# The first batch's attention heads in whole float32 products instead of split ones

## Chip, cores, metric

One core of one Trainium2 chip. The metric is the device time of one execution in microseconds, lower is better.

## What is computed

Block-causal attention over 8 batches of 8 heads (576 positions, 64 dimensions), then, per batch, the real part of a two-dimensional Fourier transform added to the attention's output, a normalization and a two-layer network with ReLU:

```python
scores = scale * np.matmul(q, k.transpose(0, 1, 3, 2))
scores = np.where(mask, scores, -1000000000.0)      # mask: 64-blocks, causal
attn = np.exp(scores - np.max(scores, axis=-1, keepdims=True))
attn = attn / (np.sum(attn, axis=-1, keepdims=True) + 1e-09)
out = np.matmul(attn, v)
...
X = np.fft.fft(np.fft.fft(x, axis=1), axis=2)
u = x + np.real(X)
un = (u - mu) / np.sqrt(var + 1e-06)
return u + np.maximum(un @ w_ch1, 0.0) @ w_ch2
```

q, k and v are float32, the network's weights float64.

## The kernel before

No product is done in float32 as such. An operand is split into a leading part and what is left, each in a type that TensorE takes in one pass, and the products of the parts are added in PSUM.

- **Scores.** `load_head` brings q and k of a head (64 rows, 1152 columns) into a tile `raw`. `lead` (ScalarE) rounds them to float32r in a tile `LEAD`, which also holds eight rows of a mask and a ninth for the row maxima. `rest` subtracts, q's half on VectorE and k's on GpSimd, into a tile `REST` of 128 rows, whose other halves get copies of the lead parts by two DMAs (`lead_copies`). `max_part` multiplies lead by lead with the mask (72 rows) for the row maxima, `shift` turns the maxima on TensorE and puts them by DMA into row 73 of `LEAD`, and `scores` makes each piece of the scores, transposed, as a product of `REST` (128 rows) plus one of `LEAD` (73 rows).
- **Probabilities.** ScalarE takes the exponential twice, into f16 (`ph`) and into float32 (`p32`); GpSimd subtracts to make the low part `pl`.
- **Values.** V of a pair of heads is scaled by a power of two from its sum of squares (`sum_v`, `split_v`, with a product by a matrix of ones on TensorE) and split into f16 parts `VH` and `VL`. `values` makes 15 blocks a head, each as three f16 products: `ph` with `VH`, `ph` with `VL`, `pl` with `VH`. VectorE then normalizes into `x`, and a DMA stores it to a scratch tensor `xd`.

`NB = 3` heads have `LEAD` and `REST` tiles at a time. When all eight heads of a batch are in `xd`, its transform starts: `mirror` gathers rows by DMA, `fourier_steps` does the rest, and `feed_steps` the network in f16 parts. The network's float64 weights are loaded by DMAs that ScalarE issues, `weight_single` turns them into float32 by bit operations on VectorE (`W`), and `weight_parts` makes f16 parts; for the first matrix ScalarE and GpSimd do this, and it waits for the scale of the whole matrix. Heads of batch 1 and later wait until the first matrix is ready.

The order of instructions on each engine is set when the program is built: a planner takes steps from several lanes (`head_lane`, `prepare_lane`, `v_lane`, `max_lane`, `score_lane`, `value_lane`, `transform_lane` and the weights' lanes), each step with a cost on TensorE and a chain of costs on other engines, and writes out the one that is due next. Each engine then runs its instructions in that order. All products are recorded at lines L216 and L219, all other engines' work at L194.

Of the kernel before, what the change touches and what calls it, by code (L numbers as in the profile page):

```python
# [200 lines left out]
def tile_attn_fourier_ffn(  # L201
# [43 lines left out]


    NB = 3
    LEAD = [const.tile([KS, 64 + 2 * S], F32R, name=f"lead{i}") for i in range(NB)]
# [3 lines left out]
    VH = [const.tile([P, 5, 2, D + 1], F16, name=f"VH_{i}") for i in range(2)]  # L252
    VL = [const.tile([P, 5, 2, D], F16, name=f"VL_{i}") for i in range(2)]
    ZT = const.tile([34, NCOS], F32R, name="ZT")
    for i in range(NB):
        gpsimd.dma_start(LEAD[i][D:KS], c_masks)
        vector.tensor_scalar(LEAD[i][0:D, 0:64], ones[0:D, 0:64], 0.0, None, op0=ALU.mult)
    for i in range(2):
        vector.memset(VH[i][:, 0:4, :, D:D + 1], 1.0)
        vector.memset(VH[i][0:64, 4, :, D:D + 1], 0.0)  # L260
        vector.memset(VH[i][64:128, 4, :, D:D + 1], 1.0)
# [90 lines left out]

    def load_head(h):

        raws[h] = work.tile([D, 2 * S], F32, name="raw", bufs=2)
        sync.dma_start(raws[h], qk[h])
        yield

    def lead(h):
        scalar.copy(LEAD[h % NB][0:D, 64:], raws[h])  # L360
        yield

    def lead_copies(h):
# [12 lines left out]
        yield  # L376

    def load_v(g):
        V = vraw[g] = work.tile([P, 5, 2, D], F32, name="V", bufs=1)
        sync.dma_start(V.rearrange("p c h d -> p (c h d)"), v[g])  # L380
        yield

    vraw = {}
# [9 lines left out]
    def split_v(g):  # L393

        acc = vsums.pop(g)
        V = vraw.pop(g)
        t = ps_tile()
        mm(t[:, 0:1], ones, acc[:, 0:1], start=True, stop=True)
        yield
        sc = acc[:, 2:3]  # L400
        x = work.tile([P, 1], I32, name="pw", bufs=2)
        vector.tensor_copy(acc[:, 1:2], t[:, 0:1])
        vector.tensor_scalar(
            x, acc[:, 1:2].bitcast(I32), 0x7F000000, 1, op0=ALU.bitwise_and, op1=ALU.logical_shift_right
        )
# [3 lines left out]
        scalar.activation(vh[:, :, :, 0:D], V, AF.Copy, scale=sc)  # L409
        yield  # L410
        vector.scalar_tensor_tensor(vl, V, sc, vh[:, :, :, 0:D], op0=ALU.mult, op1=ALU.subtract)
        pairs[g] = sc
        yield

    def head_lane():
        for h in range(B * H):
            yield Step(
                lambda: load_head(h), 0.0, ("Q0.6", "M1.0", "L2.0"), (("T2", h - 2, 0), ("T2", h - 2, 1)) if h > 1 else (), ("L", h), place=h - 2.2
            )

    def prepare_lane():
        for h in range(B * H):
            yield Step(
                lambda: lead(h), 0.0, ("A1.15",), (("L", h),), ("T", h), place=h - 1.0,
                need=(("S", h - NB, 2),) if h >= NB else (),
            )
            yield Step(lambda: lead_copies(h), 0.0, ("Q1.2", "M1.0", "L1.6"), (("T", h),), ("TC", h), place=h - 0.9)
            yield Step(lambda: rest(h, 0), 0.0, (_x(S),), (("T", h),), ("T2", h, 0), place=h - 0.8)
            yield Step(lambda: rest(h, 1), 0.0, (_g(S),), (("T", h),), ("T2", h, 1), place=h - 0.8)

    def v_lane():
        for g in range(B * H // 2):
            yield Step(
                lambda: load_v(g), 0.0, ("Q0.6", "M1.1", "L2.0"), (("N", g - 1),) if g else (), ("LV", g), place=2 * g - 2.2,
            )
            yield Step(lambda: sum_v(g), 0.0, ("t1", "A0.95", "t"), (("LV", g),) + ((("V", 2 * g - 3, 4),) if g > 1 else ()), ("NS", g),
                       place=2 * g - 0.6)
            yield Step(
                lambda: split_v(g), 0.11, ("D0.46", "B", "A0.83", "X0.88"), (("NS", g),), ("N", g), True,
                need=(("V", 2 * g - 3, 4),) if g > 1 else (), place=2 * g - 0.4,  # L440
            )

    def max_part(h, n):

        m = M[h % 2]
        x = LEAD[h % NB][0:KM]
        kh = x[:, 64 + S:]
        qh = lambda j: x[:, P * j:P * (j + 1)]
# [23 lines left out]
    def shift(h):  # L472

        t = ps_tile()
        tp(t[0:5, 0:P], M[h % 2][:, 0:5], ident)
        yield
        mt = work.tile([5, P], F32R, name="mt", bufs=2)
        scalar.activation(mt, t[0:5, 0:P], AF.Copy, bias=float(8.0 * PSHIFT * np.log(2.0)), scale=-1.0)
        yield
        dst = LEAD[h % NB][KM:KS, 0:640].rearrange("r (j p) -> r j p", j=5)  # L480
        sync.dma_start(dst.bitcast(F32), mt.bitcast(F32))
        yield

    probs = {}
# [9 lines left out]
    def scores(h, n):  # L494
# [2 lines left out]
        i, at, chunks = PIECES[n]  # L497
        if at == 0:
            width = S if i == 0 else 512
            probs[h, i] = [work.tile([P, width], F16, name=f"p{x}{i}", bufs=1) for x in "hl"]  # L500
        ph, pl = probs[h, i]
        t = ps_tile()
        w = 0
        for c, lo, width in chunks:
            first, last = P * c + lo, P * c + lo + width
# [16 lines left out]
    def values(h, at):  # L522
# [8 lines left out]
        ph, pl = probs[h, tile_]  # L531
        for j in range(c, 5):

            lo = col + P * (j - c) - (64 if j == 4 else 0)
            for i, (lhs, rhs, w) in enumerate((
                (ph, vh[:, c, hh], D + 1), (ph, vl[:, c, hh], D), (pl, vh[:, c, hh], D + 1)
            )):
# [13 lines left out]
        den, sc = DEN[h % 2], pairs[g]  # L551
        eps = 1e-9 * 2.0 ** PSHIFT
        vector.tensor_scalar(den, av[:, :, D], eps, sc, op0=ALU.add, op1=ALU.mult)
        rec = work.tile([P, 5], F32, name="rec", bufs=2)
        vector.reciprocal(rec, den)
        vector.tensor_tensor(
            x[:, :, hh], av[:, :, 0:D], rec.unsqueeze(2).to_broadcast([P, 5, D]), op=ALU.mult
        )
        yield
        if hh == 1:  # L560
# [7 lines left out]
    def score_lane():  # L568
        for h in range(B * H):
            for n, (i, at, chunks) in enumerate(PIECES):  # L570
                w = sum(x[2] for x in chunks)
                yield Step(
                    lambda n=n: scores(h, n), w / 1200.0, (_a(w), "p1", _a(w), "B", _g(w), "p"),
                    (("X", h), ("TC", h), ("T2", h, 0), ("T2", h, 1)), ("S", h, i) if n else None, True,
                    need=(("V", h - 1, 2 * i),) if h else (), place=h,
                )

# [373 lines left out]
    def weight_load(x):  # L951

        i, n, at = LANDS[x]
        if x < 2:
            vector.tensor_copy(raw(x)[0:1, 0:1].bitcast(F32), raws[x][0:1, 0:1])
            yield
        scalar.dma_start(raw(x).rearrange("p (j n) -> p j n", j=n), weight(i, n))
        yield
# [52 lines left out]
    def load_lane():  # L1011

        for x, (i, n, at) in enumerate(LANDS):
# [1 line left out]
            after = tuple(("WS", y) for y in {x - FLIGHT, *same} if y >= 0) + ((("WL", x - 1),) if x else ())  # L1015
            yield Step(
                lambda: weight_load(x), 0.0, (("D0.2",) if x < 2 else ()) + ("A0.45", f"M{1.8 * n}", "L2.0"),
                (("LV", 0), ("L", x)) if x < 2 else after, ("WL", x),
            )

    def weight_lane(w):
# [147 lines left out]
```

## Time and profile before

| | |
|---|---|
| median of 3 runs | 1278.12 us (1277.02 to 1279.54) |
| span of the profiled execution | 1275.3 us, 25121 instructions |
| that execution's own time | not given apart from its span |
| TensorE products | 1181.1 us busy (93%) |
| VectorE, ScalarE, GpSimd | 703.5 (55%), 548.7 (43%), 523.6 us (41%) |
| mean granted TensorE clock | 0.947 |
| first batch's heads, batch 0's transform, the rest | to about 93 us, to about 172 us, to the end |

In the profile's rows PE is a product on TensorE, PEld a load of its stationary operand, DVE VectorE, ACT ScalarE, POOL GpSimd, SP the queue that issues most DMAs. A product's row starts when it begins to stream and ends when its results are out, so neighbouring rows overlap, and the distance of starts is what a product costs in a row of them.

### The profile page before, as it was taken

What the parts mean: (1) busy time and instruction counts of PE and PEld (TensorE: products, weight loads), DVE (VectorE), ACT (ScalarE), POOL (GpSimd) and SP (SyncE); (2) the same over time, 40 slices, a digit from 0 to 9 for tenths busy, and PEclk for the clock granted to TensorE, in tenths of its full rate; (3) what the DMA queues carried; (4) which work ended last, traced back from release to release, by engine and by line L of the source; (5) the groups of instructions that cost most, each with busy time, mean ns of one, the idle gap of its engine ahead of it and who ended that gap; (6) DMA issues with size and microseconds to landing.
All of it is one profiled execution on the core that took longest, in us unless ns stands there. A gap on an engine that the chain in (4) does not pass through costs nothing.

```text
span 1275.3 us, 25121 instructions
## 1 busy us (share of the span) xinstructions
PE 1181.1 (93%) x10068; PEld 892.9 (70%) x10068; DVE 703.5 (55%) x1433; ACT 548.7 (43%) x1137; POOL 523.6 (41%) x593
## 2 busy tenths in 40 slices
PE   5772598999799999999999999999999999999998
PEld 5672376677677777777777777777777667766665
DVE  6787777756747574664546573557445414422211
ACT  5655647554444555534645545454443112111110
POOL 4664944454643654563534644446441400300000
PEclk9655688999899999999999999999999999999999
DMA  7674242342223233232323232413220100000000
GB/s 210 201 243 156 80 140 70 87 111 52 74 71 109 62 81 86 79 75 54 93 75 95 65 90 68 111 51 87 77 74 10 40 19 19 21 17 1 17 17 17
DMA packets 56371, 99.07 MB, mean 78 GB/s; under 512 B 7757, under 2 KB 26653, under 8 KB 56256
## 3 DMA queue, kind: packets, MB, share of 16 engines
q1 hardware_dynamic: 49152, 73.16, 21.2%
q10 hardware_dynamic: 4384, 16.78, 4.0%
q0 software_dynamic: 2720, 7.54, 2.1%
q8 instruction: 79, 1.29, 0.4%
q14 instruction: 36, 0.29, 0.1%
HBM read 58.46 MB, written 18.87 MB: 61 GB/s over the span
## 4 chain that ended last, share of the span: by engine, by line
PE 80%; DVE 10%; POOL 3%; issue 3%; DMA 2%; ACT 1%; SPq 0%; DVEq 0%; POOLq 0%; ACTq 0%
PE acc L216 28%; PE h L216 27%; PE ps L216 17%; PE av L216 6%; DVE W L194 2%; DVE M L194 2%; DVE tmp L194 2%; PE ps L219 2%; POOL u L194 1%; DMA lead<-mt 1%; DVE VL L194 1%; POOL W L194 1%; POOL pl L194 1%; DVE rest L194 1%; POOL ag L194 0%
## 5 line engine op out<-in xcount | busy, mean ns | idle before, releaser
L216 PE MATMUL h<-uh,W 128*128 128x256 f16 x2304 | 431.4, 275 | 2.7 <-DVE M L194 2.3
L194 POOL TENSOR_TENSOR pl<-p,ph 128x288 f16<-128x288 f32 (+1 forms) x256 | 253.7, 1002 | 355.6 <-ACT p L194 167.8
L216 PEld LDWEIGHTS <-W 128*128 128x128 f16 x3456 | 325.8, 99 | 64.9 <-issue 6.3
L216 PE MATMUL acc<-W,gh 128*128 128x512 f16 x1104 | 329.8, 380 | 0.0
L216 PE MATMUL h<-ul,W 128*128 128x256 f16 x1152 | 315.8, 274 | 0.0
L194 DVE TENSOR_REDUCE M<-ps 128x1 f32<-128x448 f32 (+3 forms) x292 | 131.9, 484 | 181.3 <-PE ps L216 180.5
L194 ACT ACTIVATE gh<-h 128x512 f16<-128x512 f32 x138 | 82.3, 597 | 305.1 <-PE h L216 302.3
L216 PE MATMUL ps<-lead 72*128 72x64 f32 (+9 forms) x700 | 201.3, 346 | 9.2 <-ACT lead L194 6.8
L216 PE MATMUL acc<-W,gl 128*128 128x512 f16 x552 | 209.2, 379 | 0.0
L194 DVE SCALAR_TENSOR_TENSOR gl<-h,gh 128x512 f16<-128x512 f32 x138 | 94.6, 687 | 200.9 <-ACT gh L194 200.8
L194 ACT ACTIVATE ph<-ps 128x512 f16<-128x512 f32 (+1 forms) x233 | 117.5, 506 | 146.9 <-PE ps L216 144.3
L216 PEld LDWEIGHTS <-gh 128*128 128x128 f16 x1104 | 96.7, 98 | 80.1 <-issue 4.7
L216 PEld LDWEIGHTS ps<-lead 72*128 72x128 f32 (+1 forms) x700 | 128.0, 202 | 18.3 <-ACT lead L194 6.8
L216 PEld LDWEIGHTS <-ph 128*128 128x128 f16 x1920 | 113.5, 104 | 31.1 <-ACT left L194 4.9
L216 PE MATMUL ps<-rest 128*128 128x320 f32 (+3 forms) x350 | 124.0, 361 | 1.4 <-ACT p L194 0.8
L216 PE MATMUL av<-VH,ph 128*128 128x65 f16 x960 | 118.1, 203 | 6.1 <-DVE x L194 6.1
L194 ACT ACTIVATE p<-ps 128x512 f32<-128x512 f32 (+1 forms) x233 | 117.2, 505 | 4.3 <-POOL pl L194 2.8
L216 PE MATMUL av<-VH,pl 128*128 128x65 f16 x960 | 116.6, 201 | 1.8 <-POOL pl L194 1.4
L216 PE MATMUL av<-VL,ph 128*128 128x64 f16 x960 | 117.2, 201 | 0.0
L194 POOL TENSOR_TENSOR rest<-raw,lead 64x576 fp32r<-64x576 f32 x64 | 96.9, 1514 | 15.1 <-ACT lead L194 9.5
L216 PEld LDWEIGHTS <-gl 128*128 128x128 f16 x552 | 54.0, 98 | 66.2 <-DVE gl L194 1.7
L216 PEld LDWEIGHTS <-pl 128*128 128x128 f16 x960 | 94.8, 103 | 2.7 <-POOL pl L194 2.5
(169 smaller groups left out, 1435.4 us busy)
## 6 DMA issues: line engine op xcount, KB each, us to landing
raw<-in_qk_dram SPq DMA_DIRECT2D x64, 288.0 KB
rest<-lead SPq DMA_DIRECT2D x128, 144.0 KB
W<-in_moe_w_ch_dram ACTq DMA_DIRECT2D x14, 1024.0 KB
V<-in_v_dram SPq DMA_DIRECT2D x32, 320.0 KB
xd<-x SPq DMA_DIRECT2D x32, 256.0 KB
out_dram<-u SPq DMA_DIRECT2D x32, 256.0 KB
u<-xd SPq DMA_DIRECT2D x8, 512.0 KB
u<-in_moe_w_ch_dram ACTq DMA_DIRECT2D x4, 512.0 KB
```

What stands on the lines that cost most here:

```text
L194: x = f(*args, **kw)
L216: return tc.keep_in_program_order(nc.tensor.matmul(*args, **kw))
L219: return tc.keep_in_program_order(nc.tensor.transpose(*args, **kw))
```

## The change

For the eight heads of batch 0 alone, `h < H`:

- q and k are loaded straight into `LEAD`, now a float32 tile; `lead` writes their float32r rounding into `REST`, with masks of its own, and `max_part` works on that. No rest is made and nothing copied.
- `scores` is one float32 product a piece, 73 rows; one exponential in float32, no `pl`.
- V is loaded by two DMAs straight into a float32 tile with one column of ones, which both heads of a pair share; no scale, no split. `values` is one float32 product a block, and `DEN` needs no scale.

From head 8 on the kernel is as before; its `LEAD` tiles are taken anew as float32r in the same place (masks loaded and 64 columns filled again), f16 probabilities and V parts lie in the same bytes as the float32 ones, and the columns of ones are written again.

```diff
+    def lead_tile(i, kind):
+        x = work.tile([KS, 64 + 2 * S], kind, name=f"lead{i}", bufs=1)
+        LEAD[i:i + 1] = [x]
+        gpsimd.dma_start(x[D:KS], c_masks)
+        vector.tensor_scalar(x[0:D, 0:64], ones[0:D, 0:64], 0.0, None, op0=ALU.mult)
...
+        lead_tile(i, F32)
+        gpsimd.dma_start(REST[i][D:KM, 0:S], c_masks[0:KM - D, 64 + S:])
+        gpsimd.dma_start(REST[i][D:KM, S:], c_masks[0:KM - D, 64:64 + S])
...
+        if h < H:
+            sync.dma_start(LEAD[h % NB][0:D, 64:], qk[h])
...
     def lead(h):
-        scalar.copy(LEAD[h % NB][0:D, 64:], raws[h])
+        if h < H:
+            turned = REST[h % NB][0:D].rearrange("p (t s) -> p t s", t=2)[:, ::-1]
+            scalar.copy(turned, LEAD[h % NB][0:D, 64:].rearrange("p (t s) -> p t s", t=2))
+        else:
+            if h < H + NB:
+                lead_tile(h % NB, F32R)
+            scalar.copy(LEAD[h % NB][0:D, 64:], raws[h])
...
+            for hh in range(2):
+                at = hh * (D + 1)
+                sync.dma_start(VF[g % 2][:, :, at:at + D], v[g].rearrange("p (c h d) -> p c h d", c=5, h=2)[:, :, hh])
...
+                need=(("S", h - NB, 2),) if NB <= h < H else (),
...
+            for c, lo, width in chunks:
+                first = P * c + lo
+                keys = 64 + S + (P * c if c < 4 else S - P)
+                mm(
+                    t[:, w:w + width], x1[:, keys:keys + P], x1[:, 64 + first:64 + first + width], start=(w == 0),
+                    stop=(c == chunks[-1][0]), skip_group_check=True,
+                )
+                w += width
+            yield
+            scalar.activation(probs[h, i][0][:, at:at + w], t[:, 0:w], AF.Exp, scale=0.125)
...
+                mm(
+                    av[:, j], probs[h, tile_][0][:, lo:lo + P], VF[g % 2][:, c, of:of + D + 1], start=(at == 0 and j == 0),
+                    stop=(at == 4), skip_group_check=True,
+                )
...
-                    lambda n=n: scores(h, n), w / 1200.0, (_a(w), "p1", _a(w), "B", _g(w), "p"),
+                    lambda n=n: scores(h, n), w / (1200.0 if h >= H else 600.0),
...
-                    lambda n=n: values(h, n), 0.09 * (5 - c), ("D0.95",) + (("Q1.2",) if h % 2 else ()) if n == 4 else (),
+                    lambda n=n: values(h, n), (0.09 if h >= H else 0.2) * (5 - c), ("D0.95",) + (("Q1.2",) if h % 2 else ()) if n == 4 else (),
```

How instructions stand changes with it. TensorE around the first scores, before (`rest` and `lead` are the tiles of head 0, `ps`, `h` and `acc` are PSUM banks, the bank's name alone tells where a product goes):

```order
L216 MATMUL h<-rest_87 128x288
L216 MATMUL h<-lead_84 128x288
L216 MATMUL ps<-rest_87 128x288
L216 MATMUL ps<-lead_84 128x288
L216 MATMUL acc<-rest_87 128x448
L216 MATMUL acc<-lead_84 128x448
L216 MATMUL acc<-rest_87 128x64
L216 MATMUL acc<-lead_84 128x64
L216 MATMUL acc<-rest_87 128x320
L216 MATMUL acc<-lead_84 128x320
L216 MATMUL acc<-rest_87 128x192
L216 MATMUL acc<-lead_84 128x192
```

and now, TensorE at the same place, with the values of head 0 (`p` the probabilities, `V` the float32 tile) right behind:

```order
L216 MATMUL ps<-lead_94 128x288 x2
L216 MATMUL ps<-lead_94 128x448
L216 MATMUL ps<-lead_94 128x64
L216 MATMUL h<-lead_94 128x320
L216 MATMUL h<-lead_94 128x192
L219 MATMUL h<-ident,M_87 5x128
L216 MATMUL av<-V_91,p_195 128x65 x5
L216 MATMUL av<-V_91,p_205 128x65 x5
L216 MATMUL av<-V_91,p_211 128x65 x5
```

Six products stand where twelve stood, and 15 for the values where there were 45; all three heads' first maxima now stand ahead of these scores, where two did.

GpSimd where the stage ends, before (`W<-p,W` makes a low part of a weight, `u<-xd,rows` is the gather of the transform):

```order
L194 TENSOR_TENSOR pl_1115<-p_1148,ph_1114 128x512
L194 TENSOR_TENSOR pl_1124<-p_1169,ph_1123 128x512
L194 MEMSET ul 128x1
L194 TENSOR_TENSOR W<-p_1231,W 128x512
L194 TENSOR_TENSOR W<-p_1237,W 128x512
L194 DMA u<-xd,rows 128x512 x2
```

and now, on GpSimd too:

```order
L194 TENSOR_TENSOR rest_86<-raw,lead_596 64x576
L194 DMA dft<-in_c_dft_dram 128x1290
L194 TENSOR_TENSOR W<-p_705,W 128x512
L194 TENSOR_TENSOR W<-p_725,W 128x512
L194 TENSOR_TENSOR W<-p_754,W 128x512
L194 TENSOR_TENSOR W<-p_762,W 128x512
L194 DMA u<-xd,rows 128x512 x2
```

Four weights' low parts stand ahead of the gather instead of two, and two fewer behind it.

VectorE at head 7's normalization (`DEN`, `rec`, `x`), before, with the conversion of a weight and the split of V ahead of it:

```order
L194 SCALAR_TENSOR_TENSOR W<-W 128x1024 x2
L194 COPY vacc<-ps 128x1
L194 TENSOR_SCALAR pw<-vacc 128x1
L194 TENSOR_SCALAR vacc<-pw 128x1
L194 TENSOR_REDUCE wst<-ul 128x1
L194 SCALAR_TENSOR_TENSOR VL_96<-V,vacc,VH_94 128x640
L194 TENSOR_SCALAR DEN_93<-av,vacc 128x5
```

and now, on VectorE:

```order
L194 COPY vacc<-ps 128x1
L194 TENSOR_SCALAR pw<-vacc 128x1
L194 TENSOR_SCALAR vacc<-pw 128x1
L194 MEMSET V_91 128x8
L194 MEMSET V_91 64x2 x2
L194 SCALAR_TENSOR_TENSOR V_91<-V,vacc,V_91 128x640
L194 TENSOR_SCALAR DEN_90<-av 128x5
```

The last conversion of the first matrix now stands ahead of head 5's normalization, and the sum of the squares of its parts (`wst<-ul`) ahead of head 6's.

More of the change, by code (lines that the diff above doesn't have):

```diff
@@ L247, in tile_attn_fourier_ffn @@
     NB = 3
-    LEAD = [const.tile([KS, 64 + 2 * S], F32R, name=f"lead{i}") for i in range(NB)]
+    LEAD = []
+    def lead_tile(i, kind):
[3 more added lines that the diff above has]
+        vector.tensor_scalar(x[0:D, 0:64], ones[0:D, 0:64], 0.0, None, op0=ALU.mult)
     REST = [const.tile([P, 2 * S], F32R, name=f"rest{i}") for i in range(NB)]
@@ L251, in tile_attn_fourier_ffn @@
     DEN = [const.tile([P, 5], F32, name=f"DEN_{i}") for i in range(2)]
-    VH = [const.tile([P, 5, 2, D + 1], F16, name=f"VH_{i}") for i in range(2)]
-    VL = [const.tile([P, 5, 2, D], F16, name=f"VL_{i}") for i in range(2)]
+    VF = [const.tile([P, 5, 2 * D + 1], F32, name=f"V_{i}") for i in range(2)]
+    halves = [x.rearrange("p c n -> p (c n)").bitcast(F16) for x in VF]
+    VH = [x[:, 0:10 * (D + 1)].rearrange("p (c h d) -> p c h d", c=5, h=2) for x in halves]
+    VL = [x[:, 10 * (D + 1):].rearrange("p (c h d) -> p c h d", c=5, h=2) for x in halves]
     ZT = const.tile([34, NCOS], F32R, name="ZT")
     for i in range(NB):
-        gpsimd.dma_start(LEAD[i][D:KS], c_masks)
-        vector.tensor_scalar(LEAD[i][0:D, 0:64], ones[0:D, 0:64], 0.0, None, op0=ALU.mult)
+        lead_tile(i, F32)
+        gpsimd.dma_start(REST[i][D:KM, 0:S], c_masks[0:KM - D, 64 + S:])
+        gpsimd.dma_start(REST[i][D:KM, S:], c_masks[0:KM - D, 64:64 + S])
     for i in range(2):
-        vector.memset(VH[i][:, 0:4, :, D:D + 1], 1.0)
-        vector.memset(VH[i][0:64, 4, :, D:D + 1], 0.0)
-        vector.memset(VH[i][64:128, 4, :, D:D + 1], 1.0)
+        vector.memset(VF[i][:, 0:4, D:D + 1], 1.0)
+        vector.memset(VF[i][0:64, 4, D:D + 1], 0.0)
+        vector.memset(VF[i][64:128, 4, D:D + 1], 1.0)
     for at in range(0, NCOS, P):
@@ L353, in load_head @@
     def load_head(h):
-        raws[h] = work.tile([D, 2 * S], F32, name="raw", bufs=2)
-        sync.dma_start(raws[h], qk[h])
+        if h < H:
+            sync.dma_start(LEAD[h % NB][0:D, 64:], qk[h])
+        else:
+            raws[h] = work.tile([D, 2 * S], F32, name="raw", bufs=2)
+            sync.dma_start(raws[h], qk[h])
         yield
     def lead(h):
-        scalar.copy(LEAD[h % NB][0:D, 64:], raws[h])
+        if h < H:
+            turned = REST[h % NB][0:D].rearrange("p (t s) -> p t s", t=2)[:, ::-1]
+            scalar.copy(turned, LEAD[h % NB][0:D, 64:].rearrange("p (t s) -> p t s", t=2))
+        else:
+            if h < H + NB:
+                lead_tile(h % NB, F32R)
+            scalar.copy(LEAD[h % NB][0:D, 64:], raws[h])
         yield
@@ L378, in load_v @@
     def load_v(g):
-        V = vraw[g] = work.tile([P, 5, 2, D], F32, name="V", bufs=1)
-        sync.dma_start(V.rearrange("p c h d -> p (c h d)"), v[g])
+        if g < H // 2:
+            for hh in range(2):
+                at = hh * (D + 1)
+                sync.dma_start(VF[g % 2][:, :, at:at + D], v[g].rearrange("p (c h d) -> p c h d", c=5, h=2)[:, :, hh])
+        else:
+            V = vraw[g] = work.tile([P, 5, 2, D], F32, name="V", bufs=1)
+            sync.dma_start(V.rearrange("p c h d -> p (c h d)"), v[g])
         yield
@@ L409, in split_v @@
         scalar.activation(vh[:, :, :, 0:D], V, AF.Copy, scale=sc)
+        if g < H // 2 + 2:
+            vector.memset(vh[:, 0:4, :, D:D + 1], 1.0)
+            vector.memset(vh[0:64, 4, :, D:D + 1], 0.0)
+            vector.memset(vh[64:128, 4, :, D:D + 1], 1.0)
         yield
@@ L426, in prepare_lane @@
             )
+            if h < H:
+                continue
             yield Step(lambda: lead_copies(h), 0.0, ("Q1.2", "M1.0", "L1.6"), (("T", h),), ("TC", h), place=h - 0.9)
@@ L432, in v_lane @@
         for g in range(B * H // 2):
+            first = g < H // 2
             yield Step(
-                lambda: load_v(g), 0.0, ("Q0.6", "M1.1", "L2.0"), (("N", g - 1),) if g else (), ("LV", g), place=2 * g - 2.2,
-            )
+                lambda: load_v(g), 0.0, ("Q1.2" if first else "Q0.6", "M1.1", "L2.0"), (("N", g - 1),) if g else (), ("N" if first else "LV", g), place=2 * g - 2.2,
+                need=(("V", 2 * g - 3, 4),) if 1 < g < H // 2 else (),
+            )
+            if first:
+                continue
             yield Step(lambda: sum_v(g), 0.0, ("t1", "A0.95", "t"), (("LV", g),) + ((("V", 2 * g - 3, 4),) if g > 1 else ()), ("NS", g),
@@ L445, in max_part @@
         m = M[h % 2]
-        x = LEAD[h % NB][0:KM]
-        kh = x[:, 64 + S:]
-        qh = lambda j: x[:, P * j:P * (j + 1)]
+        if h < H:
+            x, at = REST[h % NB][0:KM], S - 64
+            kh = x[:, 0:S]
+        else:
+            x, at = LEAD[h % NB][0:KM], 0
+            kh = x[:, 64 + S:]
+        qh = lambda j, at=at: x[:, at + P * j:at + P * (j + 1)]
         t = ps_tile()
@@ L499, in scores @@
             width = S if i == 0 else 512
-            probs[h, i] = [work.tile([P, width], F16, name=f"p{x}{i}", bufs=1) for x in "hl"]
+            pf = work.tile([P, width], F32, name=f"p{i}", bufs=1)
+            probs[h, i] = (pf,) if h < H else (pf.bitcast(F16)[:, 0:width], pf.bitcast(F16)[:, width:])
+        t = ps_tile()
+        if h < H:
+            w = 0
+            for c, lo, width in chunks:
[8 more added lines that the diff above has]
+            scalar.activation(probs[h, i][0][:, at:at + w], t[:, 0:w], AF.Exp, scale=0.125)
+            yield
+            return
         ph, pl = probs[h, i]
-        t = ps_tile()
         w = 0
@@ L550, in values @@
         xd, x = xs[b], xs["pair"]
-        den, sc = DEN[h % 2], pairs[g]
+        den = DEN[h % 2]
         eps = 1e-9 * 2.0 ** PSHIFT
-        vector.tensor_scalar(den, av[:, :, D], eps, sc, op0=ALU.add, op1=ALU.mult)
+        if h < H:
+            vector.tensor_scalar(den, av[:, :, 0 if of else D], eps, None, op0=ALU.add)
+        else:
+            vector.tensor_scalar(den, av[:, :, D], eps, pairs[g], op0=ALU.add, op1=ALU.mult)
+        of = 1 if of else 0
         rec = work.tile([P, 5], F32, name="rec", bufs=2)
@@ L954, in weight_load @@
         if x < 2:
-            vector.tensor_copy(raw(x)[0:1, 0:1].bitcast(F32), raws[x][0:1, 0:1])
+            vector.tensor_copy(raw(x)[0:1, 0:1].bitcast(F32), LEAD[x][0:1, 64:65])
             yield
@@ L1017, in load_lane @@
                 lambda: weight_load(x), 0.0, (("D0.2",) if x < 2 else ()) + ("A0.45", f"M{1.8 * n}", "L2.0"),
-                (("LV", 0), ("L", x)) if x < 2 else after, ("WL", x),
+                (("N", 0), ("L", x)) if x < 2 else after, ("WL", x),
             )
```

14 lines of the change are left out of this document (9 added, 5 removed).

## The prediction

> **What bounds the kernel now.** I read the page's busy slices first, then a table of stages, then TensorE's order of time inside the stage that the change touches.
>
> ```profile
> PE   5772598999799999999999999999999999999998
> DVE  6787777756747574664546573557445414422211
> PEclk9655688999899999999999999999999999999999
> 0.00:18.70 18.70, 5.46 (x18) 4.25 (x19) 12.85 (x38) 6.09 (x9) 5.49 (x10) 1.00 0.90 245
> 18.70:93.40 74.70, 61.81 (x512) 55.60 (x511) 60.02 (x107) 48.02 (x103) 49.81 (x50) 0.63 0.72 218
> 93.40:171.90 78.50, 34.95 (x187) 26.69 (x188) 61.42 (x92) 45.02 (x85) 52.74 (x58) 0.63 0.38 120
> 339.20:1275.30 936.10, 928.24 (x7986) 690.57 (x7983) 456.58 (x969) 359.46 (x754) 337.84 (x395) 1.00 0.21 58
> ```
>
> A stage row has start:end, its length, busy time of PE, weight loads, VectorE, ScalarE and GpSimd, the granted clock, DMA share and GB/s. From 339 us TensorE is busy 928 of 936 us, so it is full to the end. The first batch's heads, the only ones changed, run in 0 to 93 us, and there nobody is full: VectorE has 72.9 of 93.4 us. What later stages need (batch 0's transform) starts when head 7 is done, so a shift of that moment goes into the total nearly one for one.
>
> **TensorE's real speed in that stage.**
>
> ```profile
> 18.77 0.44 PE L216 MATMUL ps<-rest 128*128 128x288 f32 x1
> 19.01 0.44 PE L216 MATMUL ps<-lead 73*128 73x288 f32 x1
> 19.25 0.57 PE L216 MATMUL acc<-rest 128*128 128x448 f32 x1
> ...
> 21.33 1.16 PE L216 MATMUL ps<-lead 72*128 72x64 f32 x4
> 22.29 1.00 PE L216 MATMUL h<-lead 72*128 72x448 f32 x2
> 23.09 0.28 PE L216 MATMUL av<-VH,ph 128*128 128x65 f16 x1
> ...
> 23.89 0.24 PE L216 MATMUL av<-VH,pl 128*128 128x65 f16 x1
> 23.95 0.59 PE L216 MATMUL ps<-rest 128*128 128x288 f32 x1
> ...
> 35.29 0.41 PE L216 MATMUL h<-rest 128*128 128x448 f32 x1
> 35.54 0.36 PE L216 MATMUL h<-lead 73*128 73x448 f32 x1
> 35.74 0.20 PE L216 MATMUL h<-rest 128*128 128x64 f32 x1
> 60.00:70.00 10.00, 8.96 (x80) 8.36 (x80) 3.92 (x14) 7.33 (x16) 7.10 (x9) 0.50 0.86 268
> 120.00:124.10 4.10, 3.92 (x15) 3.25 (x16) 3.81 (x9) 2.03 (x6) 0.00 (x0) 0.50 0.00 0
> 124.20:126.00 1.80, 1.07 (x7) 0.63 (x5) 1.63 (x5) 0.80 (x2) 0.00 (x0) 1.00 0.00 0
> ```
>
> Read the starts. A 288-column product takes 0.24 us, 1.2 columns per ns; at 35.54 a 448-column one takes 0.20 us, near twice that. So before 35 us TensorE runs at half clock, although the column of granted clock says 1.00 there (its first record comes later), and at 60 to 70 us the record itself says 0.50 with TensorE busy 9 of 10 us. In this stage it is nearly always at half clock. All durations below are half-clock ones. They come from the profiled span, 1275.3 us; the runs' median is 1278.12, so 2.8 us lie around the span, and I add my difference to the median.
>
> **What the change removes.** Per head: a second exponential, the subtractions that make the low parts, two rest subtractions, two copies by DMA; per pair of heads the whole split of V.
>
> ```profile
> L194 POOL TENSOR_TENSOR pl<-p,ph 128x288 f16<-128x288 f32 (+1 forms) x32 | 34.5, 1093 | 27.6 <-ACT p L194 22.9 <-issue 4.1 <-POOL rest L194 0.2
> L194 POOL TENSOR_TENSOR rest<-raw,lead 64x576 fp32r<-64x576 f32 x9 | 15.9, 1768 | 7.7 <-ACT lead L194 7.3
> L194 DVE TENSOR_TENSOR rest<-raw,lead 64x576 fp32r<-64x576 f32 x9 | 9.3, 1037 | 1.0 <-ACT lead L194 1.0
> L194 DVE SCALAR_TENSOR_TENSOR VL<-V,vacc,VH 128x640 f16<-128x640 f32 x4 | 5.4, 1339 | 0.0
> ```
>
> GpSimd loses about 34.5 + 8 x 1.77 = 48.6 us, VectorE 8 x 1.04 + 5.4 = 13.7 of its 72.9. That is worth up to about 15 us if VectorE stays the busiest, and nothing if TensorE becomes it.
>
> **What it adds on TensorE: values.** Three f16 products for each of 15 blocks become one float32 product.
>
> ```profile
> L216 PEld LDWEIGHTS ps<-vacc,ones x58: 186/190/333, 27.0 to 931.9; 128*128 128x128 f32 x58
> L216 PEld LDWEIGHTS h<-vacc,ones x6: 316/332/333, 8.2 to 157.7; 128*128 128x128 f32 x6
> L194 DVE TENSOR_SCALAR pw<-vacc x32: 153/153/156, 10.3 to 934.0; 128x1 int32<-128x1 int32 x32
> 27.01 0.55 PEld L216 LDWEIGHTS ps<-vacc,ones 128*128 128x128 f32 x2
> 27.44 0.13 PEld L219 LDWEIGHTS acc<-ident,M 128*5 128x5 f32 x1
> ```
>
> The nearest whole-float32 product is the one by a matrix of ones: 58 + 6 = 64 weight loads for 32 pairs of heads, so each float32 product is two instruction pairs with a 128-column load each, and the two take 27.44 - 27.01 = 0.43 us. Before, 15 f16 products run from 23.09 to 23.95, 0.86 us, 45 in 2.5 us a head. After, the loads set the pace: 15 x 0.43 = 6.5 us, +4.0 a head. That is also the lower end; the upper is that loads don't hide behind the 65 columns: 2 x 65 / 1.2 = 0.11 us a pair more, 15 x 0.65 = 9.7 us. I take 6.5, since the loads of neighbouring products do overlap in the rows shown (19.01 and 19.25 are one stream apart).
>
> **Scores.** Two single-pass products over 1600 columns a head become one float32 product. Lower end: its two instruction pairs stream each column once, as rest and lead do now: 3200 / 1.2 = 2.7, with short pieces waiting for loads 3.0 us, no change. Upper end: the moving operand is split as the weights are, each pair streams every column twice, 6400 / 1.2 = 5.3, with the loads of the 64-column piece (0.43 against 0.21) 5.5 us. No row has a wide float32 product. I take 5.5: with the weights in two parts, a full product needs both parts of the other side against each, and the plan in the code charges a column just twice what it charged for the pair. By the Trainium skill ("FP8 and Floating Point Precision", TensorE Precision Notes) true float32 makes four passes through the array; no run here shows it yet, and by it the sum is the one I take.
>
> **The sum.**
>
> ```profile
> 15.18 0.38 PE L219 MATMUL h<-ident,M 128*5 128x128 f32 x1 [2.83 <-DVE M L194]
> 18.36 0.61 PE L216 MATMUL h<-lead 73*128 73x288 f32 x1 [2.50 <-DMA lead<-mt]
> 92.52 0.24 PE L216 MATMUL av<-VH,pl 128*128 128x65 f16 x1
> 96.09 0.88 DVE L194 SCALAR_TENSOR_TENSOR VL<-V,vacc,VH 128x640 f16<-128x640 f32 x1 [0.49 <-ACT VH L194]
> 96.89 0.22 DVE L194 TENSOR_SCALAR DEN<-av,vacc 128x5 f32<-128x5 f32 x1
> 97.89 3.44 DMA xd<-x
> 150.49 2.25 POOL L194 TENSOR_TENSOR W<-p,W 128x512 f16<-128x512 f32 x2
> ```
>
> Head 0's scores start when its maxima land, 18.4 us; their chain (load, cast, maxima, transpose, DMA) is as before, and the six more mask DMAs on GpSimd end before the cast that is waited for. From there TensorE has 8 x (5.5 + 6.5) = 96, six heads' maxima (heads 3 to 8) at 23.09 - 21.33 = 1.76, 10.6, seven transposes of maxima at about 0.3 (the row's 0.38 has its drain in it), 2.0, and two products by ones, 0.9: 109.5 us, ending at 127.9. Before it ended at 92.6: +35.3. A head now costs TensorE 13.7 us, and what it must wait for is shorter: VectorE's rest, 59.2 us for the stage, hides; the load of head h+3, which must now wait for the scores of head h because it goes straight into their tile, has three heads, 40 us, for load, cast, maxima and DMA; the exponential of a piece runs under the next piece; the loads of V in 256-byte pieces, which no row prices, hide in the same slack. The tiles that heads 8 to 10 take anew (a mask DMA on GpSimd each, a small fill) and the ones written again into V's tiles lie on engines that have just become emptier; I cost them at nothing, and were GpSimd full behind the gather, three DMA issues would be some 2 us.
>
> Part comes back. Head 7's normalization waited 4.4 us (92.5 to 96.9) behind weight conversion and VL on VectorE; with VectorE waiting for TensorE this goes, -4.3. The low halves of the FFN weights on GpSimd: four instead of two now stand ahead of the transform's gather, 2.25 us less in the full stretch behind it, -2.3. In all +35.3 - 4.3 - 2.3 = +28.7: 1278.1 + 28.7 = 1306.8, I say 1307. With the values' upper end 8 x 3.2 = 25 us more.
>
> **Rivals.** *A, the clock rises* (the one on the other side). TensorE has less idle time after the change, so its clock could be granted in full. Then a head costs about 6.9 us, TensorE would need 55 us from 18.4, and the stage goes back to VectorE: 59.2 us at the old busy share 0.78 is 76 us for 0 to 93, so up to -17, less the little that is no longer saved at its end: 1262. It decides if over half of this work runs at full clock: 109.5 - 81 us (what is there up to the old end, with the 6.6 us given back) is 28.5 of the 55 to be saved. For it: at 120 to 124 dense products with all 128 rows brought 1.00. Against it: 60 to 70 us, 9 of 10 busy and 0.50; and the new products fill the array less, scores with 73 rows of 128, values with 0.11 of each 0.21 us streaming. The Trainium skill ("TensorE: Matmul & The Clock Gate", What's actually happening) lets sustained activity of about 3.4 us release the clock; by that rule A holds. The trace disagrees so far: from 18.77 to 35.29 TensorE hardly pauses and keeps half clock.
>
> *B, two streams instead of four.* Scores stay at 3.0 us: 20 us less, 8 x 2.5, so +8.7: 1287.
>
> *C, a mixed clock:* dense scores raise it at times, values keep it or lose it; a third to a half of the stage at full clock gives +0 to +12, 1285.
>
> **How the numbers follow.** My forecast (half clock, four streams) 0.60, its own range 1298 to 1324; A 0.16; B 0.10; C 0.14. The range 1268 to 1324 holds most of the forecast, B, C and a part of A. About 0.2% is what a measurement can tell. Faster: A and a little of C, 0.18; within 0.2%: 0.03 of C; slower: 0.79.
>
> **What would show it.** In the changed profile: head 7's last product near 128 us and TensorE busy without gaps from 18 us, clock 0.50; score products of 288 columns as two records 0.48 us apart; value products 0.43 us apart; VectorE and GpSimd half idle; nothing changed behind but the shift. Wrong would be: a clock of 1.00 in 20 to 90 us, score records 0.24 us apart, or loads that cost more than 0.21 us.

## The result and the profile after

The changed kernel takes 1307.77 us (median of 4 runs, 1307.15 to 1308.62) against 1277.57 (1276.48 to 1279.54) for the kernel before on the same chip: ratio 1.0233, 95% interval 1.0218 to 1.0247, so 30.2 us slower. The profiled span went from 1275.3 to 1305.8 us, +30.5. The forecast was 1307, range 1268 to 1324.

First the busy slices of the changed kernel's page, then its table of stages (columns as in the table shown of before: start:end, length, busy time of PE, weight loads, VectorE, ScalarE, GpSimd, granted clock, DMA share, GB/s):

```profile
PE   6999357899999999999999999999999999999998
DVE  4442778776565765665544755576556415412211
PEclk9999967899999999999999999999999999999999
18.70:132.30 113.60, 109.33 (x383) 91.43 (x383) 47.19 (x103) 38.95 (x73) 8.95 (x15) 1.00 0.49 145
132.30:210.30 78.00, 36.50 (x229) 29.23 (x230) 61.49 (x92) 43.52 (x86) 53.48 (x62) 0.80 0.35 108
378.00:1305.80 927.80, 918.03 (x7857) 680.72 (x7855) 451.67 (x952) 347.55 (x736) 329.35 (x385) 1.00 0.22 58
```

The first batch's heads now last to 132.3 us, and TensorE is busy 109.3 of 113.6 us there; VectorE fell to 47.2, GpSimd from some 50 to 9. What follows is the old picture, later: from 378 us TensorE is full again. The clock of 1.00 in the first stage is an empty record, as in the kernel before: the first record comes at 158 us. The real clock is read from the starts on TensorE, and these are half-clock ones:

```profile
18.87 4.07 PE L216 MATMUL ps<-lead 73*128 73x288 f32 x8 [1.75 <-DMA W<-in_moe_w_ch_dram]
22.73 2.02 PE L216 MATMUL h<-lead 73*128 73x320 f32 x4
24.55 0.42 PE L219 MATMUL h<-ident,M 128*5 128x128 f32 x1
24.76 6.50 PE L216 MATMUL av<-V,p 128*128 128x65 f32 x30
31.06 1.27 PE L216 MATMUL acc<-lead 73*128 73x288 f32 x2
L216 PEld LDWEIGHTS av<-V,p x240: 286/333/337, 24.5 to 132.0; 128*128 128x128 f32 x120
```

Head 0's scores take 24.55 - 18.87 = 5.68 us. The eight records of the first row are four products, two of 288 columns, one of 448, one of 64, and take 22.73 - 18.87 = 3.86 us. With four streams of each column at 1.2 columns per ns the first three come to 4 x 1024 / 1.2 = 3.41, the short one by its two loads to 0.43: 3.84. So a float32 product is two records, and each takes the time of streaming its columns twice. The values take 31.06 - 24.76 = 6.30 us for 30 records, 0.21 each, though 65 columns stream in 0.05, and twice in 0.11. The last row counts the weight loads of all eight heads, 240, two for each of 120 products.

The end of the stage and the start of batch 0's transform, before and after (rows of the time line; the gather `u<-xd,rows` is the transform's first work on GpSimd):

```profile
104.91 1.17 POOL L194 DMA_INDIRECT u<-xd,rows  x1 [1.57 <-DMA u<-xd]
```

```profile
128.00 4.51 PE L216 MATMUL av<-V,p 128*128 128x65 f32 x20
132.55 0.16 DVE L194 TENSOR_SCALAR DEN<-av 128x5 f32<-128x5 f32 x1 [2.05 <-PE av L216]
133.49 0.93 SPq L194 DMA_DIRECT2D xd<-x  x2
136.94 1.17 POOL L194 DMA_INDIRECT u<-xd,rows  x1 [3.68 <-DMA xd<-x]
```

VectorE now waits for TensorE at head 7 (2.05 us) and normalizes at once. The store of head 7 is 133.49 - 97.89 = 35.6 us later than before, the gather 32.0, the end 30.5.

### The profile page after: what moved, and what is told of

It is laid out like the page before. It is cut to its first block, busy times and chain, and to the rows that moved or that the text cites. A ratio compares the mean times of both kernels' runs of the same rounds, so it can differ in the third digit from the quotient of the medians.

```text
span 1305.8 us, 24745 instructions
## 1 busy us (share of the span) xinstructions
PE 1230.2 (94%) x9940; PEld 928.1 (71%) x9940; DVE 685.5 (52%) x1418; ACT 528.7 (40%) x1093; POOL 479.3 (37%) x562
## 3 DMA queue, kind: packets, MB, share of 16 engines
q1 hardware_dynamic: 52544, 70.80, 20.7%
HBM read 58.70 MB, written 18.87 MB: 59 GB/s over the span
## 4 chain that ended last, share of the span: by engine, by line
PE 84%; DVE 7%; POOL 3%; issue 2%; ACT 1%; DMA 1%; SPq 0%; DVEq 0%; POOLq 0%; ACTq 0%
PE acc L216 29%; PE h L216 28%; PE ps L216 17%; PE av L216 9%; DVE W L194 2%; PE ps L219 1%; DVE M L194 1%; POOL p L194 1%; POOL u L194 1%; DMA lead<-in_qk_dram 1%; DVE tmp L194 1%; POOL U L194 1%; ACT p L194 1%; DMA W<-in_moe_w_ch_dram 0%; POOL W L194 0%
## 5 line engine op out<-in xcount | busy, mean ns | idle before, releaser
L194 POOL TENSOR_TENSOR p<-p,p 128x288 f16<-128x288 f32 x224 | 223.2, 1009 | 310.1 <-ACT p L194 158.8
L194 ACT ACTIVATE p<-ps 128x288 f16<-128x288 f32 (+2 forms) x448 | 197.9, 505 | 194.0 <-PE ps L216 187.5
L194 DVE TENSOR_REDUCE M<-ps 128x2 f32<-128x128 f32 (+3 forms) x285 | 129.6, 486 | 167.6 <-PE ps L216 167.2
L216 PE MATMUL ps<-lead 73*128 73x288 f32 (+9 forms) x693 | 206.1, 361 | 11.8 <-DVE lead L194 5.7
L216 PE MATMUL av<-V,p 128*128 128x65 f16 (+2 forms) x2760 | 160.0, 215 | 3.9 <-POOL p L194 2.1
L216 PEld LDWEIGHTS ps<-lead 73*128 73x128 f32 (+1 forms) x693 | 128.4, 204 | 28.9 <-ACT p L194 7.2
L216 PE MATMUL ps<-rest 128*128 128x288 f32 (+4 forms) x342 | 119.9, 364 | 11.9 <-ACT rest L194 6.9
L216 PEld LDWEIGHTS <-p 128*128 128x128 f16 x2520 | 98.5, 99 | 23.0 <-POOL p L194 3.5
L216 PEld LDWEIGHTS ps<-rest 128*128 128x128 f32 (+1 forms) x342 | 67.5, 200 | 23.0 <-ACT rest L194 6.9
L194 ACT CAST lead<-raw 64x1152 fp32r<-64x1152 f32 x56 | 64.1, 1145 | 0.0
L216 PE MATMUL ps<-dft,fs 128*128 128x290 f32 (+5 forms) x246 | 40.8, 314 | 19.4 <-ACT fs L194 18.2
```

The lines of the kernel that those rows point to most:

```text
L194: x = f(*args, **kw)
L216: return tc.keep_in_program_order(nc.tensor.matmul(*args, **kw))
```

## The experiments

A set's kernels are compared with runs of the kernel before on the same chip, by the ratio. Those runs took 1279.14 us (median) for the values' columns, the values alone and the first two clock experiments, 1281.03 for the kernel with the most idle products, and 1282.09 (1276.73 to 1285.51) for all others. The span before, 1275.3 us, is that of one execution, so a span of another set set against it can be off by some 5 us. "Stage end" below is the start of head 7's normalization (`DEN`): 96.9 us before, 132.5 after.

**What the values cost: loads or columns.** The change as it is, but each value product has 33 columns instead of 65, which leaves out half of every head's value columns.

```diff
-                    av[:, j], probs[h, tile_][0][:, lo:lo + P], VF[g % 2][:, c, of:of + D + 1], start=(at == 0 and j == 0),
+                    av[:, j, 0:33], probs[h, tile_][0][:, lo:lo + P], VF[g % 2][:, c, of + (0 if of else 32):of + (33 if of else D + 1)], start=(at == 0 and j == 0),
```

> The changed kernel, but each value product of batch 0 streams 33 columns instead of 65 (half of each head's value columns are left out and the other half is written twice). Theory L (a float32 product's two loads of 128 columns set its pace): value records stay 0.213 us apart, 15 products 6.4 us, total 1305 to 1311. Rival S (loading and streaming add up, 0.107 + 0.107): records 0.16 us apart, 1.6 us a head less, total about 1295.

Measured: 1309.10 us (1307.79 to 1310.15), ratio 1.0230 (1.0213 to 1.0247), as the change itself. TensorE's order of time in this kernel:

```profile
25.05 6.45 PE L216 MATMUL av<-V,p 128*128 128x33 f32 x30
31.31 1.31 PE L216 MATMUL acc<-lead 73*128 73x288 f32 x2
```

30 records in 31.31 - 25.05 = 6.26 us against 6.30. Half the columns save nothing, so the columns do not set the values' pace. The product by ones that the prediction shows took the same 0.43 us for its two loads, with a single column. That the loads are what costs is the reading that is left; no run changes them alone.

**Each half alone.** Values in float32, scores and their rests as before; then scores in float32, values in three f16 products as before.

```diff
-            scalar.copy(turned, LEAD[h % NB][0:D, 64:].rearrange("p (t s) -> p t s", t=2))
+        scalar.copy(LEAD[h % NB][0:D, 64:], raws[h])
...
```

(values alone; all of `load_head`, `lead`, `rest`, `max_part`, `scores` as before the change)

```diff
-            probs[h, i] = (pf,) if h < H else (pf.bitcast(F16)[:, 0:width], pf.bitcast(F16)[:, width:])
+            probs[h, i] = [work.tile([P, width], F16, name=f"p{x}{i}", bufs=1) for x in "hl"]
...
```

(scores alone; `load_v`, `sum_v`, `split_v`, `values` and both exponentials as before the change)

> Whole-float32 values alone: scores from rest and lead as before, with their subtractions and copies. Theory T (TensorE at half clock bounds the stage): 18.9 + 8 x (3.0 + 6.4) + 13.5 = 108 us, some waits, stage end near 111 us against 132.5 in the changed kernel and 92.6 before: total 1283 to 1292. Rival W (the stage is long because the load of a head now waits for earlier scores): this kernel has the old loads, so it should be no slower than before, 1278 or less.

> Whole-float32 scores alone: no rests and no copies, but values from f16 parts as before, with the second exponential, the low parts and the split of V. Theory T (TensorE at half clock sets the stage, plus the waits that stood in it before): 18.9 + 8 x (5.7 + 2.5) + 13.5 = 98 us and 0 to 12 us of waits, head 7's last product at 98 to 110 against 92.6 before and 132.5 in the change: total 1282 to 1297. Rival E (scores and values each carry half of the loss): about 1293. Rival V (values carry all of it, since scores cost only streams that would hide): 1278 or less.

Measured: values alone 1304.98 us, ratio 1.0205 (1.0188 to 1.0222); scores alone 1302.77, ratio 1.0158 (1.0133 to 1.0183). Values alone misses its expectation upwards, by 13 us; rival W is out too, since this kernel has the old loads and is slower all the same. Scores alone misses its own in microseconds, but on a chip where the kernel before is 4.5 us longer; its stage ends at 109.5, inside the 98 to 110. For the values TensorE's waits in the stage (total, times, longest) and head 7's normalization show why:

```profile
PE acc L216 <- DMA lead<-mt: 6.9, 1, 6.9
PE h L216 <- DMA lead<-mt: 5.6, 1, 5.6
122.96 0.17 DVE L194 TENSOR_SCALAR DEN<-av 128x5 f32<-128x5 f32 x1 [8.32 <-PE av L216]
```

The scores still need two parts, copies and the maxima by DMA, and TensorE waits 12.5 us for maxima, 5.6 of them ahead of head 0's scores, which I had left out. The stage end moves by 122.96 - 96.89 = 26.1, the span by 26.4. In scores alone the stage ends 12.6 us later, but its span is 26.5 us longer than the one before:

```profile
109.54 0.22 DVE L194 TENSOR_SCALAR DEN<-av,vacc 128x5 f32<-128x5 f32 x1 [2.00 <-PE av L216]
164.82 1.11 PE L219 MATMUL ps<-ident,un 128*128 128x128 f32 x4 [17.64 <-DVE un L194]
```

In its order the network's first transpose of batch 0 stands on TensorE 17.6 us ahead of its data; in the kernel before the longest such wait was 2.9. But the wait for the transform's `fs` ahead of it is shorter than before (15.7 us in total, before 22.3), and a second thing differs behind the stage, the granted clock (columns as in the table of stages; scores alone, the kernel before with 36 idle products from the last experiment below, and the kernel before):

```profile
349.50:366.50 17.00, 13.45 (x86) 10.77 (x87) 11.60 (x27) 5.08 (x13) 8.96 (x13) 0.50 0.21 53
329.10:346.10 17.00, 11.95 (x71) 9.82 (x71) 12.28 (x24) 6.77 (x14) 9.25 (x13) 0.50 0.24 68
332.40:339.10 6.70, 3.60 (x26) 3.55 (x27) 4.73 (x11) 1.92 (x4) 2.36 (x4) 0.50 0.32 88
```

From its stage end to the end of its span scores alone takes 1192.3 us, the kernel before 1178.4, and the kernel before with 36 idle products, whose order behind the stage is the old one and which ran on the same chip as scores alone, 1187.9. So 9.5 of the 13.9 us come without the new order, and some 4 are left for the gap; that is not tested further. Against its own chip scores alone loses 20.7 us (1302.77 - 1282.09), 12.6 of them at the stage end. The scores themselves cost 44.8 us of TensorE in the stage, as in the change (44.9). The two halves cannot be added.

**Is it the clock?** In the kernel after, 36 idle products (f16, 128 rows, 256 columns, their bank is overwritten behind them) ahead of head 0's scores; in a second kernel also one of 187 columns behind each value product.

```diff
+        if h == 0 and n == 0:
+            busy = ones.bitcast(F16)
+            for _ in range(36):
+                mm(t[:, 0:256], busy[:, 0:P], busy, start=True, stop=True, skip_group_check=True)
```

```diff
+                busy = ones.bitcast(F16)
+                mm(fulls[h][:, 5 * (D + 1):512], busy[:, 0:P], busy[:, 0:512 - 5 * (D + 1)], start=False, stop=False, skip_group_check=True)
```

> The changed kernel with 36 unused f16 products of 128 rows and 256 columns ahead of head 0's scores (7.7 us at half clock). Theory F (what raises the clock is how full the array is, rows times streaming; once up it holds while TensorE has no long gaps): the clock is granted in full about 25 us into the span and stays for much of the stage, the stage ends at 80 to 100 us, total 1262 to 1280. Rival H (half clock belongs to this part of the run, whatever TensorE does): clock 0.50 to the stage's end, 5 us lost, total about 1313.

> As the one before, and behind each float32 value product of batch 0 one unused f16 product of 187 columns into spare columns of the same bank, so that the array streams for about 0.37 of 0.47 us at half clock. Theory F: full clock from about 25 us to the stage's end, records of value products 0.107 us apart, stage end 75 to 90 us, total 1258 to 1272. Rival H: clock 0.50 and 120 more products of 0.05 to 0.16 us: total 1315 to 1330.

Measured: once, 1293.56 us (1291.33 to 1297.39), ratio 1.0112 (1.0086 to 1.0139); kept, 1306.58, ratio 1.0202 (1.0180 to 1.0225). Theory F missed both, by 13 and by 34 us; rival H is out for the first and its range starts 8 us above the second. Once, by time on TensorE and by windows:

```profile
16.84 5.61 PE L216 MATMUL ps<-ones 128*128 128x256 f16 x36
22.29 2.06 PE L216 MATMUL ps<-lead 73*128 73x288 f32 x8
24.18 1.08 PE L216 MATMUL h<-lead 73*128 73x320 f32 x4
25.10 0.27 PE L219 MATMUL h<-ident,M 128*5 128x128 f32 x1
25.21 3.46 PE L216 MATMUL av<-V,p 128*128 128x65 f32 x30
28.50 0.70 PE L216 MATMUL acc<-lead 73*128 73x288 f32 x2
42.98 0.58 PE L216 MATMUL h<-rest 72*128 72x64 f32 x3 [1.00 <-ACT rest L194]
21.00:43.80 22.80, 21.80 (x154) 19.12 (x151) 14.28 (x27) 10.79 (x21) 0.69 (x2) 1.00 0.70 214
43.80:79.00 35.20, 31.47 (x109) 25.73 (x108) 18.27 (x38) 11.29 (x20) 1.31 (x5) 0.50 0.63 184
```

The full clock comes at 19.9 us, 3.1 us after the first dense product, and head 0's scores and values then take 25.10 - 22.29 = 2.81 and 28.50 - 25.21 = 3.29 us, about half of 5.68 and 6.30. The clock falls at 43.8 us, behind value products and a wait of 1.0 us, and does not come back in the stage. I had expected it to last. The stage ended at 118.2 us instead of 132.5. Products behind every value product held the clock to 46.5 us only and cost at half clock what it had won: the stage ended at 127.7.

**Idle products only where the array was empty.** The 36 again, and 12 ahead of the turning of the maxima of heads 2 to 7, 8 ahead of the maxima of heads 3 to 7; in a further kernel 20 and 14 instead of 12 and 8 for the later heads.

```diff
+        if 3 <= h < H and n == 0:
+            busy = ones.bitcast(F16)
+            for _ in range(8):
+                mm(t[:, 0:256], busy[:, 0:P], busy, start=True, stop=True, skip_group_check=True)
...
+        if 2 <= h < H:
+            busy = ones.bitcast(F16)
+            for _ in range(12):
+                mm(t[:, 0:256], busy[:, 0:P], busy, start=True, stop=True, skip_group_check=True)
```

```diff
-            for _ in range(8):
+            for _ in range(8 if h < 6 else 14):
...
-            for _ in range(12):
+            for _ in range(12 if h < 4 else 20):
```

> The kernel with 36 unused f16 products ahead of head 0's scores, and 12 more ahead of each transpose of maxima (heads 2 to 7) and 8 ahead of each head's first maxima product (heads 3 to 7), where TensorE had its gaps. Theory F (the clock fell because a gap emptied one window): full clock holds past 44 us, through most of the stage, whose end comes at 85 to 105 us: total 1265 to 1285. Rival G (the clock falls for another reason near 44 us): it falls there again, and the 112 more products cost up to 24 us at half clock: total 1295 to 1318.

> The kernel after with idle products (f16, 128 rows, 256 columns, results overwritten): 36 ahead of head 0's scores as before, 12 ahead of the turning of the maxima of heads 2 and 3 and 20 ahead of that of heads 4 to 7, 8 ahead of the maxima of heads 3 to 5 and 14 ahead of those of heads 6 and 7. They only keep the array full where it fell under the fill that holds the clock (79 us with fewer of them). Theory H (what counts for the clock is how full the array was in the last few us): full clock to the end of the first batch's heads, last value product of head 7 at 93 to 99 us, total 1272 to 1281, ratio 0.995 to 1.003: the float32 form at full clock is worth about the old form, not more. Rival T (the clock is granted for a limited time, some 60 us, whatever is done): it falls near 80 us again, the added products then cost up to 9 us at half clock, total 1288 to 1297.

Measured: 1288.43 us (1282.70 to 1292.84), ratio 1.0049 (1.0032 to 1.0066), and with more of them 1282.73 (1277.93 to 1283.81), ratio 1.0009 (0.9993 to 1.0025). Both lie above the range of their theory, F and H, by 3.4 and 1.7 us; the second's ratio lies inside. Windows of the first, then of the second with head 7's normalization:

```profile
43.80:79.00 35.20, 32.11 (x233) 26.68 (x230) 24.36 (x49) 16.14 (x29) 1.94 (x7) 1.00 0.74 218
79.00:89.00 10.00, 10.00 (x36) 7.28 (x35) 3.22 (x6) 3.77 (x8) 2.05 (x1) 0.50 0.40 138
```

```profile
79.00:92.50 13.50, 11.83 (x86) 10.25 (x85) 8.05 (x22) 5.75 (x11) 3.25 (x4) 1.00 0.65 217
93.00:103.00 10.00, 10.00 (x39) 8.45 (x38) 1.46 (x7) 6.96 (x14) 2.97 (x3) 0.50 0.36 105
104.02 0.17 DVE L194 TENSOR_SCALAR DEN<-av 128x5 f32<-128x5 f32 x1 [2.05 <-PE av L216]
```

Full clock to 79 us in the one, to 92.6 in the other, so it is not granted for a fixed time; the last head still ran at half clock and the stage ended at 104.0, later than the 93 to 99 expected. With the clock up for most of the stage the stage end came back by 28.5 of 35.6 us (132.5 to 104.0), and by the ratio the float32 form stands level with the form before, idle products included; it does so on a chip where the form before is 3.5 us longer. From head 0's scores on, the kernel's own products take 62.3 us of TensorE instead of 109.5. The 192 idle ones take 22.6 (the sum of their distances from start to start), so about half of what the clock wins goes to what holds it.

**The same idle products in the kernel before.** The 36 alone, then the first set.

```diff
+        if h == 0 and n == 0:
+            busy = ones.bitcast(F16)
+            for _ in range(36):
+                mm(t[:, 0:256], busy[:, 0:P], busy, start=True, stop=True, skip_group_check=True)
```

> The kernel before with 36 unused f16 products ahead of head 0's scores. Theory F: full clock from about 22 us until the first longer wait; TensorE has waits in this stage, so the gain is small and the clock falls within 30 us: total 1273 to 1281. Rival (the stage before is bound by TensorE's half clock too): 1268 or less.

> The kernel before with all of the unused products: 36 ahead of head 0's scores, 12 ahead of transposes of maxima (heads 2 to 7), 8 ahead of first maxima products (heads 3 to 7). Theory F: the clock holds longer, and the stage is then set by VectorE (73 of 93 us busy): stage end 80 to 92 us, total 1266 to 1280. Rival G: the clock falls all the same and the products cost: 1280 to 1300.

Measured: 1281.84 us, ratio 0.9995 (0.9973 to 1.0017), and 1284.47, ratio 1.0014 (0.9992 to 1.0036). The first lies 0.8 us above theory F's range, the second 4.5, and the second's stage ends at 95.7 us, not at 80 to 92. The windows of the second, then head 7's normalization in the first and in the second:

```profile
21.00:43.80 22.80, 20.62 (x222) 17.38 (x219) 17.68 (x34) 15.49 (x35) 18.12 (x17) 0.93 0.53 158
43.80:79.00 35.20, 24.89 (x287) 21.80 (x286) 28.06 (x54) 22.86 (x48) 23.41 (x24) 0.89 0.84 250
```

```profile
93.85 0.22 DVE L194 TENSOR_SCALAR DEN<-av,vacc 128x5 f32<-128x5 f32 x1
95.74 0.22 DVE L194 TENSOR_SCALAR DEN<-av,vacc 128x5 f32<-128x5 f32 x1
```

A clock of 0.9 instead of 0.5 in most of this stage wins the kernel before 1.2 us at the stage end, the 36 alone, with full clock from 18.5 to 32.1 us, 3.0. So far less is to be won here than in the changed kernel. That TensorE's pace plays no part in its first stage is not shown: in the second kernel its own products from head 0's scores on fell from 62.7 to 40.8 us, but idle ones took 14.8 among them and 6.1 ahead. What sets the change apart is TensorE's waiting in that stretch: 14.8 us before, 11.0 and 14.7 in these two, 4.1 in the changed kernel. The change made TensorE the bound, and at half clock.

## Why the prediction held

- **TensorE as the new bound, at half clock: right.** It was busy 109.3 us of the stage, forecast 109.5. That the half clock is what makes it this long is shown by the idle products, not only by the spacing of starts.
- **Four streams: right.** 5.68 us a head, forecast 5.5; rival B, 3.0, is out.
- **Values at 0.43 us a product: right.** 6.30 us, forecast 6.5, and half the columns changed nothing, so the upper end of 9.7, loads and columns added up, is out.
- **"Busy without gaps": the term that was too small.** Head 7's last value product ended at 132.3, forecast 127.9. Summed from start to start: scores 44.9 (forecast 44), values 50.5 (52), maxima 12.0 (10.6), transposes and products by ones 1.8 (2.9), gaps 4.1 (none), start 0.5 later. So +0.9 - 1.5 + 1.4 - 1.1 + 4.1 + 0.5 = +4.3: nearly all of it is waits. They are these (the changed kernel's waits of TensorE, total, times, longest; the first wait for M and the one for W lie ahead of head 0's scores):

```profile
PE ps L219 <- DVE M L194: 2.6, 2, 1.3
PE ps L216 <- DMA W<-in_moe_w_ch_dram: 1.7, 1, 1.7
PE ps L219 <- DVE dft L194: 1.3, 1, 1.3
PE av L216 <- ACT p L194: 0.7, 1, 0.7
PE h L216 <- ACT rest L194: 0.7, 1, 0.7
```

- **Head 7's normalization no longer waits: right in sense and size.** 4.4 us from the last value product's start before, 0.4 now, forecast -4.3.
- **Given back behind the stage: right in sense, its size uncertain.** Forecast 2.3, measured 35.6 - 30.5 = 5.1. The gather comes 3.6 us sooner behind the store, at 3.45 instead of 7.0: before, two low parts of weights stood between the store and the gather, now all four are done ahead of the store. The forecast had put the gain behind the gather. The products that wait for the transform's `fs`, before and after:

```profile
115.13 0.61 PE L216 MATMUL h<-dft,fs 128*128 128x290 f32 x1 [19.09 <-ACT fs L194]
120.18 1.56 PE L216 MATMUL h<-dft,fs 128*128 128x290 f32 x4 [3.21 <-ACT fs L194]
```

```profile
149.24 1.41 PE L216 MATMUL ps<-dft,fs 128*128 128x290 f32 x3 [16.73 <-ACT fs L194]
152.13 0.61 PE L216 MATMUL ps<-dft,fs 128*128 128x290 f32 x1 [1.48 <-ACT fs L194]
```

  They start 17.2 and 22.3 us behind the store before, 15.7 and 18.6 now, so at most 3.7 us sooner. Where the rest of the 5.1 is won stays open, and it is within the scatter: from stage end to span end the changed kernel takes 1173.3 us, the kernels that add idle products to it 1175.1 to 1178.8, the kernel before 1178.4.
- The two errors, +4.3 and -2.8, nearly cancel: forecast +28.7, measured +30.2. That the total was closer than its terms is luck.
- **One for one:** nearly. The stage end moved by 35.6 us in the changed kernel, 26.1 with values alone, 21.3 with 36 idle products, 8.5 with more and 7.1 with the most; the span by 30.5, 26.4, 18.0, 5.6, 6.2. Scores alone (12.6 and 26.5) and the kernel before with idle products (-3.0 and +6.5, -1.2 and +8.1) break the rule; these three ran on the chip where the kernel before was longer too, and share the longer stretch of half clock behind 329 us.
- **Rival A** did not happen by itself, though its price was about right: forecast 55 us of TensorE at full clock, 6.9 a head, and a warm head measured 2.8 + 3.3 us without its maxima. The Trainium skill's rule ("TensorE: Matmul & The Clock Gate", What's actually happening), that sustained activity of some 3.4 us releases the clock, was borne out only where the array was full, by the 3.1 us of dense idle products: 113.6 us with TensorE busy 96% of them kept half clock. The Trainium skill's four passes for float32 ("FP8 and Floating Point Precision", TensorE Precision Notes) are what the scores showed, 5.68 us a head. **Rival C** did not show: in no stretch of the stage did the 0.21 us between value records turn to half.

## What to carry to other kernels

Before replacing several cheap products by fewer costly ones, price them at the clock that the stage has, by spacing of starts, and ask whether the new form fills the array enough to change it; fewer instructions and emptier vector engines were worth nothing here, since TensorE became the bound at half clock. A float32 product with few columns has a price that its columns do not lower: 0.43 us at half clock, for 65 columns as for 33. Where a stage's end starts the next, count TensorE's waits in it as a term of their own. And set a trace against one of the same chip, or compare stage ends: here the time behind the stage differs by 9.5 us between two kernels with the same order there.

## What was not expected of the hardware

In these traces the clock goes by how full the array is, not by whether TensorE is busy, and it is kept on less work than it takes to raise it. The records of granted clock change in steps of 3.41 us. For each step I worked out the share of time in which columns stream, times the share of the 128 rows in use, with two streams of the columns for each float32 record, as measured on the scores and taken to hold for the values too, and half clock ahead of the first record. The changed kernel's scores then fill 73 of 128 rows all the time, 0.57, and its values stream 2 x 65 / 1.2 = 108 of every 213 ns, 0.51; no step of its heads passes 0.58.

In the first batch's heads of all eleven kernels each of the 14 rises followed a step of 0.75 or more (0.75 to 1.01, where over 1 is the error of the sum), and none of the 238 other steps at half clock, 0.74 at most, brought one. Each of the 14 falls followed a step of 0.36 or less, and the clock stayed through all 65 steps of 0.38 or more. Products of 187 columns behind every value product fit: the clock fell behind a step of 0.33, and the later steps reach 0.72 at most. Over the first 420 us, with float32 transposes counted as two streams as well, 82 rises and 71 falls keep to nearly the same limits (0.73 or more, 0.38 or less); three steps of 0.75, 0.78 and 0.79 brought no rise. The limits were read off the traces that they describe; what the hardware itself counts is not shown.
